# Half a piece of the expert weights per head pair, the rest in and behind the last eight pairs, and row replication moved from the chain into the expert stage: attention followed by soft mixture of experts on one core

## The chip, the core and the metric

The kernel runs on one core of one Trainium2 chip. The metric is device time in microseconds (us). Engines: TensorE (PE; its weight loads are PEld), VectorE (DVE), ScalarE (ACT), GpSimd (POOL), SyncE (SP). Sixteen DMA engines move the data. A profile shows one execution; its span is about 1.8 us shorter than the time of the same run. Runs over 1.5% above the fastest of their kernel count as slow and are left out of ratios.

## The reference

Causal attention over 8 batches x 8 heads of 576 tokens, with 16 beacon keys and values ahead of them; its output, as 4608 rows of 512, goes through a soft mixture of 8 experts with 4 slots each.

```python
scores = scale * np.matmul(q, k_all.transpose(0, 1, 3, 2))     # causal mask, softmax
x = attn_out.transpose(0, 2, 1, 3).reshape(B * S, H * D)       # 4608 x 512
logits = x @ phi                                               # 4608 x 32 slots
d = softmax(logits, axis=0); slot_input = d.T @ x
for e in range(8):                                             # w1: 512 x 1024, w2: 1024 x 512
    slot_out[e] = np.maximum(slot_input[e] @ w1[e], 0) @ w2[e]
out = softmax(logits, axis=1) @ slot_out
```

The slot inputs need all rows of x, so no expert can start before the last head pair is done. The weights are 33.5 MB in 4-byte floats; q, k and v are 9.4 MB each.

## The kernel before

Attention runs over 32 pairs of heads. SyncE issues the loads of q and k, five pairs ahead. GpSimd masks the exponentials, and in the same instruction stream issues the loads of v and of the expert weights, which the transfer casts to 2-byte floats. The weights come in 32 pieces, four per expert (two of w1, then two of w2), each 128 packets of 4096 bytes in SBUF.

```python
def load_w(i):                       # ... source of piece i
    nc.gpsimd.dma_start(out=arena[:, wloc[m]:wloc[m] + WP], in_=src)

for n in range(NP):                  # 32 pairs
    ...                              # scores, exponentials, masks, products, transposes
    want = n if n < 6 else n - (n - 1) // 4 if n < 24 else 18 + 9 * (n - 23) // 5
    while wl < min(want, NPC):
        load_w(wl)
        wl += 1
while wl < NPC:
    load_w(wl)
    wl += 1
```

Each issue on GpSimd waits for the transfer eight places before it, because completions are counted on eight semaphores in turn. Behind the loop stands the tail: the last pair, the logits of the last batch, three memsets on GpSimd that clear padding, the replication of exponentials into all row groups (`spread_rows`, `spread_ends`: products and a copy), the slot inputs (`si_half`), and then the experts, two at a time:

```python
for p in range(EP + 2):              # EP = 4 pairs of experts
    if p < EP:
        first_layer(p)               # 16 products with w1
    ...
    if 0 < p <= EP:
        turn_hidden(p - 1)
    if p > 1:
        second_layer(p - 2)          # 16 products with w2
soh = ...                            # VectorE scales the slot outputs: "the scaling"
```

After the scaling come the output products, two copies out of PSUM and 9.44 MB of stores.

The softmax here doesn't subtract the row's maximum and nothing guards it: scores larger than these inputs give would overflow.

## Time and profile before

| stage (profiled run) | us |
|---|---|
| GpSimd starts its last weight issues (all masking done) | 148.8 |
| last weight packet lands | 162.7 |
| scaling starts | 166.1 |
| span | 194.7 |
| median of the first three runs | 197.3 |

Where a stage is quoted from the trace below, "scaling" is the group `soh<-av,rd` of VectorE, "second-layer products" are `av<-arena,hbuf` of TensorE, and "last weight packet" is the end of the last DMA packet of 4096 bytes in the packet records. Counts of packets, pieces and read rates are sums over the packet records (casts counted double for reads), not lines of a view.

### The profile page before, as it was taken

The page shows a single profiled execution, that of the slowest core. Times are in us where ns is not written, and L with a number is a line of the kernel's source. Part 1 is how long each engine was busy: PE and PEld are TensorE (multiplying, and loading weights), DVE is VectorE, ACT ScalarE, POOL GpSimd, SP SyncE. Part 2 cuts the span into 40 slices and gives each one's busy share as a digit, 9 for nine tenths or more (in the row PEclk, how much of TensorE's full clock was granted, in tenths as well). Part 3 has the DMA queues.
Part 4 walks back from the last instruction along what each step waited for, and adds up shares of the span by engine and source line. Part 5 has one row for each costly group of instructions (what it writes and reads, how often), then busy time and mean ns, then how long its engine had stood idle before and what let it go on. Part 6 is the DMA issues. An engine that isn't in the chain of part 4 may idle for free. (4 is left out here: it accounts for less than half of the span.)

```text
span 194.7 us, 7324 instructions
## 1 busy us (share of the span) xinstructions
PE 156.7 (81%) x3123; PEld 106.8 (55%) x3123; DVE 138.6 (71%) x286; ACT 128.3 (66%) x175; POOL 112.5 (58%) x293
## 2 busy tenths in 40 slices
PE   6778986779999888968999799988878699887400
PEld 2445765646776665646767566656656544454100
DVE  5537697578989888985799699788657342799700
ACT  2697763748997778775889678877795222578500
POOL 8659893945897597778778687666756100000000
PEclk9955899979999999996999999999999889999955
DMA  6999999999999999999999999999999990399994
GB/s 183 264 240 350 271 242 266 280 261 265 311 261 265 260 276 258 278 255 304 272 282 260 255 293 261 256 254 222 211 213 215 213 186 19 105 380 417 416 428 199
DMA packets 20464, 50.84 MB, mean 261 GB/s; under 512 B 5456, under 2 KB 5456, under 8 KB 19408
## 3 DMA queue, kind: packets, MB, share of 16 engines
q0 software_dynamic: 8048, 21.74, 56.3%
q1 hardware_dynamic: 12240, 28.35, 40.6%
q8 instruction: 24, 0.39, 0.8%
q10 hardware_dynamic: 144, 0.29, 0.5%
q14 instruction: 8, 0.07, 0.1%
HBM read 62.65 MB, written 9.44 MB: 370 GB/s over the span
## 5 line engine op out<-in xcount | busy, mean ns | idle before, releaser
L294 ACT ACTIVATE ex<-sc 128x736 f16<-128x736 f32 (+1 forms) x124 | 101.5, 870 | 27.4 <-PE sc L287 25.4
L296 POOL TENSOR_SCALAR_AFFINE_SELECT ex<-ex 128x256 f16<-128x256 f16 (+1 forms) x155 | 57.3, 399 | 31.4 <-ACT ex L294 31.0
L287 PE MATMUL sc<-qT,kT 64*128 64x336 bf16 (+5 forms) x384 | 44.9, 302 | 4.4 <-ACT ex L294 2.1
L309 PEld LDWEIGHTS <-ex 128*128 128x128 f16 (+1 forms) x930 | 37.5, 108 | 16.9 <-issue 14.8
L309 PE MATMUL av<-vh,ex 128*128 128x65 f16 x840 | 39.6, 200 | 6.3 <-issue 3.4
L270 PE MATMUL tr<-idb,arena 64*64 64x64 bf16 x1152 | 32.0, 201 | 6.6 <-DMA arena<-in_k_dram 2.3
L270 PEld LDWEIGHTS <-arena 64*64 64x64 bf16 x1152 | 25.4, 114 | 20.2 <-issue 13.3
L276 DVE COPY kT<-tr 128x576 bf16<-128x576 bf16 x27 | 20.4, 756 | 9.6 <-PE tr L270 9.6
L320 DVE TENSOR_TENSOR xb<-av,r 128x640 f16<-128x640 f32 x31 | 25.6, 825 | 1.1
L276 DVE COPY qT<-tr 128x576 bf16<-128x576 bf16 x32 | 23.2, 725 | 4.0 <-PE tr L270 3.9
L287 PEld LDWEIGHTS <-kT 64*128 64x128 bf16 (+1 forms) x384 | 15.9, 102 | 14.1 <-issue 6.1
L151 DVE STREAM_TRANSPOSE vh<-vbuf 128x256 f32<-128x256 f32 x32 | 20.4, 657 | 3.3 <-DMA vbuf<-in_beacon_v_dram 1.9
L183 POOL DMA_DIRECT2D arena<-in_moe_w_dram x32 | 17.9, 560 | 0.2
L698 ACT ACTIVATE arena<-fp,rc 128x512 f32<-128x512 f32 (+1 forms) x18 | 11.3, 677 | 7.4 <-PE fp L696 5.9
L127 POOL DMA_DIRECT2D vbuf<-in_v_dram x27 | 15.1, 571 | 0.2 <-DVE xb L320 0.2
L340 DVE COPY xT<-tr 128x592 f16<-128x592 f16 x31 | 13.9, 455 | 1.0 <-PE tr L332 1.0
L332 PE MATMUL tr<-idh,xb 128*128 128x128 f16 (+1 forms) x160 | 14.2, 221 | 0.1
L700 DVE TENSOR_SCALAR arena<-fp,rc 128x512 f32<-128x512 f32 (+1 forms) x19 | 13.1, 732 | 1.2 <-PE fp L696 0.4
L696 PE MATMUL fp<-soh,eLh 128*128 128x512 f16 (+1 forms) x37 | 10.6, 373 | 2.5 <-ACT arena L698 1.7
L319 DVE RECIPROCAL r<-av 128x10 f32<-128x10 f32 x31 | 6.8, 218 | 7.9 <-PE av L309 7.5
L332 PEld LDWEIGHTS <-xb 128*128 128x128 f16 (+1 forms) x160 | 10.4, 103 | 1.1 <-issue 0.9
L696 PEld LDWEIGHTS <-eLh 128*128 128x128 f16 x37 | 3.9, 114 | 5.7 <-issue 4.5
(101 smaller groups left out, 135.6 us busy)
## 6 DMA issues: line engine op xcount, KB each, us to landing
arena<-in_moe_w_dram POOLq DMA_DIRECT2D x32, 512.0 KB, 10.0
arena<-in_q_dram SPq DMA_DIRECT2D x32, 288.0 KB, 14.6
arena<-in_k_dram SPq DMA_DIRECT2D x31, 288.0 KB, 14.9
out_dram<-arena SPq DMA_DIRECT2D x8, 1024.0 KB, 7.2
vbuf<-in_v_dram POOLq DMA_DIRECT2D x30, 128.0 KB, 8.4
arena<-in_v_dram POOLq DMA_DIRECT2D x4, 128.0 KB, 8.4
out_dram<-arena SPq DMA_DIRECT2D x2, 256.0 KB, 3.5
out_dram<-arena SPq DMA_DIRECT2D x1, 512.0 KB, 4.0
```

The source lines that it names most:

```text
L127: nc.gpsimd.dma_start(out=vbuf[b % 2][32 * qd:32 * qd + 32, :], in_=bass.AP(tensor=v.tensor, offset=v.offset + lo, ap=[hs_, cs_, [1, TK * ...
L151: nc.vector.transpose(out=dst[:, e], in_=src.bitcast(FP).rearrange("p (j e) -> p e j", j=TK)[:, e])
L183: nc.gpsimd.dma_start(out=arena[:, wloc[m]:wloc[m] + WP], in_=src)
L270: nc.tensor.transpose(tp[po:po + 64, j, :], hi, idb[po:po + 64, po:po + 64])
L276: nc.vector.tensor_copy(out=dst, in_=src)
L287: nc.tensor.matmul(sc[0:kn, a, col:col + un], kT[n % 3][64 * a:64 * a + 64, P * c:P * c + kn], qT[n % 3][64 * a:64 * a + 64, u0:u0 + un], ...
L294: nc.scalar.activation(e, sc[:, :, 0:w], AF.Exp, scale=scale)
L296: nc.gpsimd.affine_select(out=e[0:m, :, o:o + m], in_=e[0:m, :, o:o + m], compare_op=AL.is_ge, fill=0.0, base=0, pattern=[[0, 2], [1, m]], ...
L309: nc.tensor.matmul(dst[0:m, i * DD:(i + 1) * DD], ex[n][0:kn, o + a * w:o + a * w + m], vchunk(b, 2 * g + a, c, kn), start=(c == 0), stop= ...
L320: nc.vector.tensor_tensor(out=xb[b % 2][:, :, 2 * g:2 * g + 2, :].rearrange("p i a d -> p a i d"), in0=avv[:, :, :, 0:D], in1=r5[:, :, :]. ...
L332: nc.tensor.transpose(tp[:, i, 0:m], xb[b % 2][0:m, i, 2 * g:2 * g + 2, :].rearrange("p h d -> p (h d)"), idh[0:m, 0:m])
L696: nc.tensor.matmul(fp_[:, c], etok(cg, j), soh[:, c], start=True, stop=True)
```

## The change

Two parts go together. The weight schedule issues half a piece per pair until pair 23, and the rest in the last eight pairs and behind them; its intent, as I read it, is to leave the transfers to q, k and v while attention runs. The tail moves replication out of the chain ahead of the slot inputs into the first expert pair, adds three idle products, meant to keep TensorE's clock up, and puts half of a small fold ahead of the last transposes.

```diff
-        want = n if n < 6 else n - (n - 1) // 4 if n < 24 else 18 + 9 * (n - 23) // 5
+        want = n // 2 if n < 24 else 12 + 5 * (n - 23) // 4
@@ last pair
-        if rows == (0,):
-            spread_rows(0, nc.vector)
@@ logits of the last batch
     logits(L, lp, [0, 1, 2])
-    fold_si(0)
+    xt_piece(NP - 1)
     fold_si(1)
-    xt_piece(NP - 1)
     logits(L, lp, [3])
     logit_exp(L, lp)
-    spread_rows(1, nc.scalar)
+    spread_rows(0, nc.scalar)
+    warm_tail(3)                     # three 128x512 products, result unused
     ...
-    spread_ends(0, 4, nc.scalar, av[:, 1, 128:128 + 4 * UL])
@@ experts
         if p < EP:
             first_layer(p)
+        if p == 0:
+            spread_ends(0, 4, nc.scalar, av[:, 1, 128:128 + 4 * UL])
+            spread_rows(1, nc.scalar)
```

(`fold_si(0)` now stands right after `xt_piece(NP - 2)`, ahead of the logits.)

More of the change, by code (lines that the diff above doesn't have):

```diff
@@ L602, with warm_tail @@
     lp = scs[1][:, 0, 0:ZW]
+    fold_si(0)
     logits(L, lp, [0, 1, 2])
-    fold_si(0)
+    xt_piece(NP - 1)
     fold_si(1)
-    xt_piece(NP - 1)
     logits(L, lp, [3])
     logit_exp(L, lp)
-    spread_rows(1, nc.scalar)
+    spread_rows(0, nc.scalar)
+    def warm_tail(k):
+        for _ in range(k):
+            nc.tensor.matmul(scs[0][:, 1, :], idh[:, :], xTs[L % 2][:, 0:512],
+                             start=True, stop=True)
+    warm_tail(3)
     dt_piece(L)
```

## The prediction

> **What bounds the kernel now.** I read the page first, then the windows view (busy time of each engine in chosen stretches), the list of DMA issues, the timeline from 149 us on, and last the waits of single instructions. The page gives the engines and three rows over 40 slices of 4.87 us:
>
> ```profile
> PE 156.7 (81%) x3123; PEld 106.8 (55%) x3123; DVE 138.6 (71%) x286; ACT 128.3 (66%) x175; POOL 112.5 (58%) x293
> ...
> DMA  6999999999999999999999999999999990399994
> GB/s 183 264 240 350 271 242 266 280 261 265 311 261 265 260 276 258 278 255 304 272 282 260 255 293 261 256 254 222 211 213 215 213 186 19 105 380 417 416 428 199
> ...
> q0 software_dynamic: 8048, 21.74, 56.3%
> q1 hardware_dynamic: 12240, 28.35, 40.6%
> ```
>
> No engine is full, but the 16 DMA engines are: nine tenths or more in every slice from the second to the 33rd, then a hole of two slices, then the output. q0 (the GpSimd queue) carries v and the expert weights, cast from 4-byte to 2-byte, so the GB/s of the page, which counts bytes written, is half of what is read for them; q1 carries q, k and the output. The windows view gives the stages (the last numbers of a row are the granted clock, the DMA share, and GB/s written):
>
> ```profile
> 60.00:92.00 32.00, 27.06 (x607) 19.52 (x605) 27.06 (x53) 23.48 (x30) 24.73 (x67) 0.95 1.06 272
> 92.00:129.00 37.00, 34.24 (x817) 24.39 (x813) 31.31 (x61) 30.07 (x40) 26.82 (x72) 0.99 1.06 268
> 129.00:149.40 20.40, 17.87 (x392) 12.90 (x385) 14.63 (x30) 16.24 (x21) 14.15 (x38) 1.00 1.06 217
> 149.40:166.10 16.70, 13.98 (x211) 7.60 (x210) 6.62 (x19) 4.37 (x8) 1.42 (x5) 0.90 0.70 142
> 166.10:194.70 28.60, 13.80 (x99) 7.73 (x99) 16.41 (x32) 12.88 (x23) 0.00 (x0) 0.82 0.81 331
> ```
>
> So attention ends near 149 us, the expert stage near 166, and the output is paced by its write (0.92 to 1.02 DMA share from 170 on). Within attention TensorE is busy 85 to 93% and DMA is over 1.0: two limits that nearly coincide. From about 131 us on the queue holds only weights. Counting their 4096-byte packets (128 to a 512 KB piece), ten pieces end between 133.7 and 158.5 us, **2.48 us apiece**. The last of the 32 lands near 160.5 us, 11 us after its issue at 149.4. The timeline shows what then ends the expert stage:
>
> ```profile
> 148.81 1.08 POOL L183 DMA_DIRECT2D arena<-in_moe_w_dram  x2
> ...
> 164.16 1.91 PE L665 MATMUL av<-arena,hbuf 128*32 128x512 f16 x32
> ...
> 166.13 0.88 DVE L684 TENSOR_SCALAR soh<-av,rd 128x256 f16<-128x256 f32 x2 [1.43 <-PE av L665]
> ```
>
> The last second-layer products, which read the last pieces, start at 164.16, 3.7 us after the data is there. The weights are hidden now, with 3 to 4 us to spare; the chain attention, logits, slot inputs, experts sets the end.
>
> **What the Trainium skill says.** Page "DMA: Bandwidth & Descriptors", section "Anatomy of one DMA — SWDGE (gpsimd) path": a GpSimd DMA costs about 2.0 us plus its bytes over 436 GB/s. The trace agrees on the rate, if bytes read are counted: 211 to 213 GB/s written is 422 to 426 read while only weights run. The same section says that any semaphore wait happens on the issuing sequencer before dispatch. That is why the place of an issue in GpSimd's program counts: the trace has each weight issue as 0.55 us of GpSimd's queue, behind the pair's masking. Page "TensorE: Matmul & The Clock Gate", section "Part 1: The HAM clock gate": after an idle window of about 3.4 us the clock falls to half. The trace agrees in kind (0.50 to 0.55 granted between 10 and 20 us), and it will matter if TensorE has to wait for weights.
>
> **The change part by part.**
>
> (a) *Weight schedule.* There are 32 pieces. The code before issues up to n for pairs n below 6, n-(n-1)//4 up to 23, and 18+9(n-23)//5 after: 18 by pair 23, all 32 by pair 31. After: n//2 gives 11 by pair 23, then 12+5(n-23)//4: 13, 14, 15, 17, 18, 19, 20, 22 for pairs 24 to 31, and **10 more behind the last pair**. The instruction order of GpSimd shows it: after the last masking come 12 weight issues in a row (2 of pair 31 and the 10), where before there were 2.
>
> What it removes: 7 pieces of 2.48 us = 17.4 us of DMA work from before pair 24; 3 of them lie before pair 6, where TensorE is busy only 14.9 of 20 us (24 to 44). What it adds: this work comes back at the end, where nothing is left to hide it. Pairs 24 to 30 issue 9 pieces, 22.3 us of DMA in about 28 us, with the last k and q loads as all the rest, so I take it that no backlog is left when the last pair is masked. Then, from the moment T when GpSimd is done masking (148.8 us before):
> - the first of the 12 pieces lands at about T + 0.55 (issue) + 2.0 (the skill's fixed cost, an estimate) + 2.5 = T + 5;
> - the other 11 follow at 2.48 us: 27.3 us. Last landing T + 32.3 us.
>
> With T unmoved that is 181.1. Four products and the start of the scaling by VectorE behind it: 0.5 us, so 181.6 in place of 166.1: **+15.5 us**.
>
> (b) *What attention gains, X.* Less DMA early lets v, k and q land sooner and T come earlier. The waits view has from 24 to 135 us: TensorE and its weight loads behind k and q 5.9 us, VectorE behind v 1.9, GpSimd behind v and phi 2.9; these overlap. Against a large gain: reckoning landings from the packets, q and k of pairs 9 to 30 arrive 5 to 12 us before their transposes, so the steady state is paced by TensorE and ScalarE. I choose **X = 5 us**, 1 to 10 being possible; TensorE's idle time from 24 to 149 us is 16 us in all, which no change of loads can remove whole.
>
> (c) *Rows replicated elsewhere.* Four replication products leave the last attention pair (0.4 us), seven more and two ScalarE copies (0.58 and 0.44 us) leave or move in the chain before the slot inputs, and stand in expert pair 0; three 128x512 warm products come in (about 0.2 us each at full clock), and half of the fold moves ahead of the last transposes. Between 151.5 and 155.4 us the chain could lose some 1 us, above all the 1.11 us that replicated ends wait for GpSimd's memsets. But behind (a) the experts wait for weights 20 us later, so this is worth **0** on the path. One new hazard: those memsets now stand behind the 12 issues. A piece waits for the one eight places before it, so the last issue waits for piece 24, about T + 5 + 3 x 2.48 = T + 12.5, and TensorE, in order, waits in expert pair 0. That is before the last landing at T + 32, and the remaining expert pairs (2.2 us each in the timeline) fit between.
>
> (d) *Output.* Same 9.44 MB at the same rate, 28.6 us from the scaling to the end. TensorE comes out of waits, so its first products may run at half clock: +0.5 us at most, an estimate from 0.37 us mean of an output product times a few.
>
> Sum: 15.5 - 5 + 0 + 0.2 = +10.7 on 197.3, about **208 us**.
>
> **The rivals.**
> 1. *Attention was starved by loads, and the relief pays for it all.* For: DMA share 1.06 through all of attention, TensorE at 75% in 24 to 44 us. Against: k and q land well ahead; X would have to be 14 or more, nearly all TensorE idle time. It would give 193 to 199 us.
> 2. *The weights are hidden anyway.* They have 3.7 us of slack and DMA is work-conserving, so if DMA never idles it still ends near 160.5, the chain gains 1 us of (c) and something of X: 193 to 196 us. Against: q and k have only five buffers, so removed weights can't be replaced by other loads for long; 17.4 us of work removed early leaves holes, and 12 pieces issued at T need 30 us whatever came before.
> 3. *GpSimd's queue is the bound.* The memsets behind 12 issues hold TensorE past the last landing: only if they came after T + 28. Then 210 to 214 us.
>
> **Range and chances.** The 27.3 us of the last 11 pieces are firm to half a microsecond; X is the uncertain term. X from 1 to 10 gives 203 to 212; the runs before spread from 196.0 to 200.3, so I take 202.5 to 212.5. Within 2% would need X of 11 or more: 5%; faster by 2% needs rival 1 or 2 in full: 2%; slower: 93%.
>
> **What would show it.** In the changed profile: (a) GB/s and DMA share under 0.9 in some slices before 140 us, weights alone at about 213 GB/s for some 30 us after attention, last landing near 175; TensorE's expert products waiting for the weight DMA; the hole between loads and output shrinking to some 3 us. (b) The last exponentials of attention near 144 instead of 148. (c) No row copies between the logits' exponential and the slot inputs, memsets some 12 us after the last masking. (d) 28 to 29 us from scaling to end. The prediction is wrong if DMA stays full all through attention, or if attention ends before 138.

## The result

The changed kernel takes 210.74 us (208.0 to 213.5, 4 runs) against 197.15 us: ratio 1.066, interval 1.052 to 1.081, slower. A ratio here is the mean time of one kernel's fast runs over that of the other's fast runs of the same rounds, so it isn't quite the ratio of the medians. The results are correct.

The page of the changed kernel, the same two rows over 40 slices, now of 5.22 us:

```profile
DMA  6999999999999799899999898997999998089994
GB/s 178 263 280 347 289 278 262 286 281 285 204 267 269 176 246 256 227 199 248 275 237 267 236 195 151 187 173 146 185 213 212 213 214 179 25 333 413 414 425 206
```

Before, the DMA row had nothing but nines until the output; now there are sevens and eights from slice 14 on, and slices as low as 146 and 151 GB/s. The stretch of weights alone at 212 to 214 GB/s (211 to 215 before) moved from slices 29 to 32 to slices 30 to 33 here, with longer slices and a later end. The windows view of the same stages (from the last: granted clock, DMA share, GB/s written):

```profile
60.00:92.00 32.00, 28.71 (x675) 20.83 (x673) 27.69 (x53) 25.09 (x33) 24.22 (x68) 0.99 0.94 232
92.00:129.00 37.00, 34.34 (x801) 24.46 (x797) 32.56 (x64) 30.64 (x39) 25.52 (x70) 1.00 1.00 237
149.40:180.00 30.60, 15.02 (x167) 6.29 (x164) 4.56 (x13) 3.40 (x6) 3.59 (x9) 0.67 0.95 191
180.00:208.80 28.80, 15.02 (x99) 8.02 (x98) 16.11 (x32) 13.14 (x23) 0.00 (x0) 0.80 0.80 329
```

In the first two rows the transfers write 232 and 237 GB/s where they wrote 272 and 268, and TensorE is a little busier (28.7 of 32 us against 27.1): attention did gain. In the third row TensorE works 15 of 30.6 us, with the DMA share at 0.95. The last row, the output, is as it was.

Why DMA isn't full any more is told by the waits of SyncE, which issues q and k (us in total, times, longest us). First the kernel before, then the changed one:

```profile
SPq L95 <- DMA arena<-in_q_dram: 25.9, 21, 2.9
SPq L95 <- PE tr L270: 14.3, 12, 2.1
```

```profile
SPq L95 <- PE tr L270: 42.7, 24, 4.1
SPq L95 <- DMA arena<-in_q_dram: 2.3, 4, 1.2
```

The two other large lines, for k and for TensorE's scores (`PE sc L287`), are alike: 24.5 and 14.9 us before, 1.9 and 39.2 us changed. Before, SyncE waited mostly for earlier loads to land (14.6 us from issue to landing for q in the page, 7.0 us changed). With fewer weights in the way it waits for TensorE instead, which has to be done with one of the five buffers. So q and k can't fill the freed time.

The timeline of the changed kernel around the end of the experts:

```profile
145.15 3.73 POOL L183 DMA_DIRECT2D arena<-in_moe_w_dram  x7
...
159.54 0.53 POOL L183 DMA_DIRECT2D arena<-in_moe_w_dram  x1 [1.89 <-DMA arena<-in_moe_w_dram]
160.10 0.20 POOL L616 MEMSET eLh<- 32x128 f16 x1
...
160.70 0.43 PE L367 MATMUL av<-eLh,rept 128*128 128x128 f16 x3 [9.90 <-POOL eLh L617]
...
174.04 0.40 PE L669 MATMUL av<-arena,hbuf 128*32 128x512 f16 x4 [0.59 <-DMA arena<-in_moe_w_dram]
...
176.54 0.40 PE L669 MATMUL av<-arena,hbuf 128*32 128x512 f16 x4 [2.10 <-DMA arena<-in_moe_w_dram]
...
178.95 0.62 PE L669 MATMUL av<-arena,hbuf 128*32 128x512 f16 x4 [2.01 <-DMA arena<-in_moe_w_dram]
...
179.61 0.88 DVE L691 TENSOR_SCALAR soh<-av,rd 128x256 f16<-128x256 f32 x2 [6.89 <-PE av L669]
```

The square bracket tells how long the engine idled before the group, and for whom. Two waits are to be seen. TensorE stood 9.9 us for GpSimd's memsets, which stand behind the twelve weight issues in GpSimd's stream. Later it stood 0.6, 2.1 and 2.0 us for weight pieces, one after the other. The second kind comes last. Which of the two sets the end is a question for an experiment, since the first is the longer.

### The profile page after: what moved, and what is told of

It is laid out like the page before. It is cut to its first block, busy times and chain, and to the rows that moved or that the text cites. A ratio compares the mean times of both kernels' runs of the same rounds, so it can differ in the third digit from the quotient of the medians.

```text
span 208.8 us, 7327 instructions
## 1 busy us (share of the span) xinstructions
PE 160.5 (77%) x3126; PEld 107.4 (51%) x3126; DVE 137.5 (66%) x285; ACT 129.2 (62%) x176; POOL 112.7 (54%) x293
## 5 line engine op out<-in xcount | busy, mean ns | idle before, releaser
L294 ACT ACTIVATE ex<-sc 128x736 f16<-128x736 f32 (+1 forms) x124 | 101.5, 869 | 24.5 <-PE sc L287 23.2
L287 PE MATMUL sc<-qT,kT 64*128 64x336 bf16 (+5 forms) x384 | 44.9, 298 | 4.1 <-ACT ex L294 1.5
L309 PEld LDWEIGHTS <-ex 128*128 128x128 f16 (+1 forms) x930 | 37.0, 107 | 18.2 <-issue 14.4
L309 PE MATMUL av<-vh,ex 128*128 128x65 f16 x840 | 39.0, 199 | 8.0 <-issue 3.1
L270 PE MATMUL tr<-idb,arena 64*64 64x64 bf16 x1152 | 31.3, 200 | 4.0 <-DVE qT L276 1.9
L270 PEld LDWEIGHTS <-arena 64*64 64x64 bf16 x1152 | 25.1, 113 | 16.7 <-issue 10.9
L287 PEld LDWEIGHTS <-kT 64*128 64x128 bf16 (+1 forms) x384 | 16.0, 101 | 13.3 <-issue 4.7
L705 ACT ACTIVATE arena<-fp,rc 128x512 f32<-128x512 f32 (+1 forms) x18 | 11.4, 678 | 13.1 <-PE fp L703 11.3
L707 DVE TENSOR_SCALAR arena<-fp,rc 128x512 f32<-128x512 f32 (+1 forms) x19 | 13.2, 733 | 2.1 <-PE fp L703 1.3
L703 PE MATMUL fp<-soh,eLh 128*128 128x512 f16 (+1 forms) x37 | 11.6, 415 | 2.3 <-ACT arena L705 1.7
L367 PEld LDWEIGHTS <-rept 128*128 128x128 f16 x41 | 3.2, 108 | 12.1 <-issue 11.0
```

The costliest lines, as they stand in the source:

```text
L270: nc.tensor.transpose(tp[po:po + 64, j, :], hi, idb[po:po + 64, po:po + 64])
L287: nc.tensor.matmul(sc[0:kn, a, col:col + un], kT[n % 3][64 * a:64 * a + 64, P * c:P * c + kn], qT[n % 3][64 * a:64 * a + 64, u0:u0 + un], ...
L294: nc.scalar.activation(e, sc[:, :, 0:w], AF.Exp, scale=scale)
L309: nc.tensor.matmul(dst[0:m, i * DD:(i + 1) * DD], ex[n][0:kn, o + a * w:o + a * w + m], vchunk(b, 2 * g + a, c, kn), start=(c == 0), stop= ...
```

## The experiments

My theory: the schedule takes transfer work away from a time when the DMA engines have no other work to fill in, and the same work then stands behind the last pair, where nothing hides it. The scaling comes a fixed short time behind the last weight packet. Rivals: the tail costs the time; GpSimd's stream holds TensorE (the 9.9 us); the position of the ten issues behind the last pair counts, not the work put off; attention was starved by loads and should have won far more.

### Schedule alone, tail alone

e1 is the kernel before with the one line of the schedule changed:

```diff
-        want = n if n < 6 else n - (n - 1) // 4 if n < 24 else 18 + 9 * (n - 23) // 5
+        want = n // 2 if n < 24 else 12 + 5 * (n - 23) // 4
```

> The weight schedule alone, with the tail of the kernel before. My theory (the ten pieces behind the last pair set the end): as slow as the whole change, 208 to 213 us, last weight packet about 33 us after GpSimd starts its closing issues, and first scaling by VectorE 1 us behind it. In the old tail the replicated ends stand ahead of the slot inputs, so TensorE will wait there for the memsets until about 160 us and do all experts after that, but should still be done before the last piece. Rival (the rearranged tail costs the time): near 197 us.

Measured: 210.16 us, ratio 1.072 (1.062 to 1.082). The schedule alone costs all of it. In the old tail the slot inputs also wait for the memsets, as the waits and the timeline of e1 show:

```profile
PE av L367 <- POOL eLh L612: 10.9, 1, 10.9
...
178.30 0.62 PE L665 MATMUL av<-arena,hbuf 128*32 128x512 f16 x4 [1.83 <-DMA arena<-in_moe_w_dram]
178.96 0.88 DVE L684 TENSOR_SCALAR soh<-av,rd 128x256 f16<-128x256 f32 x2 [8.07 <-PE av L665]
```

TensorE lost 10.9 us ahead of all experts and still stood waiting for the last pieces at the end.

e2 is the changed kernel with the old line of the schedule (the same edit the other way round).

> The rearranged tail alone, with the old weight schedule. My theory: it shortens the chain from the last logits to the first expert pair by about 1 us and the weights do not bind, so 195.5 to 197 us, ratio to before 0.99 to 1.00; the scaling starts at about 165 us instead of 166.1. Rival (moved copies cost as much in the expert pairs): same as before or up to 1 us slower. If the tail were the cause of the loss: over 205 us.

Measured: 195.03 us, ratio 0.987 (0.976 to 0.999); its profile fell in a slow run (mean clock 0.74, with 0.75 granted where the others have 1.0). The tail is a small gain, not the loss.

### Memsets off GpSimd

e3 takes the 9.9 us wait away and leaves all else of the changed kernel:

```diff
-    nc.gpsimd.memset(eLz[64:96, :, 4, UL - 64:32], 0.0)      # and two more
+    nc.vector.memset(eLz[64:96, :, 4, UL - 64:32], 0.0)
```

> The changed kernel with its three closing memsets on VectorE instead of behind twelve weight issues on GpSimd. Theory: TensorE's wait of 9.9 us for these memsets disappears from the trace, the experts run earlier and wait for the weights instead, and the time stays within 1% of the changed kernel, 208 to 213 us. Rival (GpSimd's queue holds the end): 5 to 10 us faster than the changed kernel, 200 to 205 us.

Measured: 210.4 us, ratio 1.068 (1.057 to 1.079), against 1.066 of the changed kernel. In its profile, which is of a slow run, the memsets run at 149.3 us and TensorE no longer waits for them; a product for the column sums waits for GpSimd's copy of the fold instead (9.2 us), which the move left behind the issues. The last packet still lands 34.8 us after the closing issues begin, and the scaling follows 0.97 us behind it. So e3 swapped one wait for GpSimd against another and doesn't rule its stream out by itself; nor does e4 below, where GpSimd is free early too. The timelines do: in the changed kernel TensorE, released by GpSimd at 160.7 us, still stood 4.7 us in all for weight pieces, the last until 178.95 us; and in e5 GpSimd had done its last work at 153.2 us, 18 us before the scaling.

### The suspected cause taken away

e4 gives a wrong result: the last ten pieces aren't loaded, and the experts that would read them read pieces loaded ten places earlier.

```diff
-    while wl < NPC:
-        load_w(wl)
-        wl += 1
+    for i in range(wl, NPC):
+        wloc[worder[i]] = wloc[worder[i - 10]]
```

> Wrong result on purpose: the changed kernel without its last ten weight loads; the experts that would read them read pieces loaded ten places earlier. It takes the suspected cause away and keeps all the arithmetic. Theory: the scaling starts about 16 us after the last masking, near 161 us, and the time is 191 to 194 us, 3 to 6 us under the kernel before, which is what attention gained plus 1 us of the tail. Rival (something else in the change lengthens the chain): 200 us or more.

Measured: 192.14 us, ratio 0.976 (0.967 to 0.986), relative error 0.82. Its timeline:

```profile
146.28 1.08 POOL L183 DMA_DIRECT2D arena<-in_moe_w_dram  x2
...
161.76 0.88 DVE L690 TENSOR_SCALAR soh<-av,rd 128x256 f16<-128x256 f32 x2 [1.43 <-PE av L668]
```

Without those ten loads the scaling comes 15.5 us after the closing issues begin instead of 34.5. All the arithmetic and all the other issues are still there. The ten pieces cost 18.6 us in the medians (210.74 less 192.14), on other chips, so take it as about 18.

### Work put off, or place behind the last pair

e5 keeps the lean schedule until pair 23 but issues all other 21 pieces within the last eight pairs.

```diff
-        want = n // 2 if n < 24 else 12 + 5 * (n - 23) // 4
+        want = n // 2 if n < 24 else 11 + 21 * (n - 23) // 8
```

> The changed kernel with its half-a-piece-per-pair schedule up to pair 23 (11 pieces), but all other 21 pieces issued in the last eight pairs, none behind. It tells whether the ten issues behind the last pair cost the time, or the transfer work that was put off. Theory (work put off, transfers then at one piece in 2.47 us): 21 pieces from about 116 us last till about 170, scaling near 171, time 201 to 205 us, ratio 1.02 to 1.04, so about half of the loss stays though nothing is issued behind the last pair. Rival (the position behind the last pair is what costs): 194 to 197 us.

Measured: 203.67 us, ratio 1.037 (1.018 to 1.057); last packet at 170.7, scaling at 171.7 us. Nothing stands behind the last pair in program order, and half of the loss is still there, so the position isn't the whole cost. GpSimd's issues now wait for their eighth predecessor, from 141.9 us on (the last starts at 151.6 us), so the transfers decide when they can be made. The other half went, and the packet records show how: all of q and k has landed by 119.3 us in the changed kernel and by 117.7 us in e5, and from 119.3 us to the closing issues the weights were then read at 337 GB/s in the changed kernel, which asks for too few, and at 423 GB/s in e5. So 9.4 pieces instead of 12.6 were left at the end. In both kernels it is the work still left after attention that costs.

### How much attention can gain

e7 loads no weight at all until the last pair is done (`want = 0`).

> The changed kernel with no weight loaded before the last pair is done: all 32 behind it. It measures how early attention can end with no weights beside it, the most that relief can give. Theory: attention is then paced by TensorE and ScalarE, and GpSimd is done masking at 141 to 145 us against 148.8 before; the 32 pieces last 79 us more, time 252 to 260 us. Rival (attention is starved by loads): masking done before 135 us.

Measured: 250.97 us in one run; all masking is done at 137.2 us, better than I expected but short of the rival's 135. The windows of e7:

```profile
60.00:92.00 32.00, 29.74 (x710) 21.66 (x706) 29.74 (x59) 26.75 (x34) 24.15 (x68) 1.00 0.75 186
92.00:129.00 37.00, 35.94 (x864) 26.48 (x863) 33.77 (x64) 32.73 (x42) 21.97 (x63) 1.00 0.40 102
```

TensorE is busy 97% of 92 to 129 us (93% before), with DMA at 0.40. So the weights slow attention by 11.6 us in all (148.8 to 137.2, one profile each); the changed schedule won back 3.7 of these, and to win all 11.6 costs 82 us of weights at the end. Which of attention's waits the weights lengthen I didn't pin down: the profile before shows only a few microseconds of waits for q, k and v.

### The clock of TensorE

In five profiles (changed kernel, e1, e5, e7, e8) TensorE waits for the last weight pieces, and its granted clock is at half when the scaling starts; there the span ends 29.2 to 29.3 us after the scaling (28.9 in the slow run of e3). In those with the full clock at the scaling (before, e4, e6, e10, e11) it is 28.2 to 28.7. e8 adds four idle products ahead of each of the last three groups of second-layer products, e9 eight:

```diff
         for z in range(4):
+            if p == EP - 1 and z > 0:
+                warm_tail(8)                     # e8: 4
```

> The changed kernel with four idle products of 128x512 ahead of each of the last three groups of second-layer products, which wait for weights about 2 us each. It tests whether TensorE's lowered clock after these waits costs the output anything. Theory: scaling starts at the same distance from the last packet (1 us or less), the clock of the first output products is back at full, and the distance from the scaling to the end falls from 29.2 to about 28.6 us. Rival (clock has no part in it): 29.2 stays.

> As the run with four idle products ahead of each wait, but eight: there the granted clock still fell to 0.50 ahead of the output and the distance from scaling to end stayed 29.3 us, so that run could not tell. Eight products at full clock fill about 1.7 us of each 2.47 us. If the clock stays at 1.0 into the output and the distance falls to about 28.6 us, the lowered clock is what costs the 0.6 us; if the clock stays at 1.0 and the distance is still 29.2 us or more, it is not; if the clock falls again, it stays open.

e8 (one look, 207.96 us) told nothing, because the clock still fell. e9 (one look, 211.62 us) did tell. The windows of e8, then of e9, around the scaling, at 176.9 and 181.7 us (first number after the stretch: TensorE busy; third from the end: granted clock):

```profile
174.00:176.00 2.00, 1.14 (x8) 0.40 (x5) 0.00 (x0) 0.00 (x0) 0.00 (x0) 0.97 0.45 90
176.00:178.00 2.00, 1.20 (x7) 0.49 (x7) 0.88 (x2) 0.14 (x1) 0.00 (x0) 0.50 0.00 0
```

```profile
178.00:180.00 2.00, 2.00 (x12) 0.83 (x12) 0.00 (x0) 0.00 (x0) 0.00 (x0) 1.00 0.55 111
182.00:184.00 2.00, 1.67 (x14) 1.08 (x14) 1.57 (x4) 1.14 (x3) 0.00 (x0) 1.00 0.00 0
```

In e9 the clock stays at 1.0 and the end comes 28.2 us after the scaling, 1.0 us less than in the changed kernel. So the lowered clock accounts for the extra half microsecond or more; but the idle products delay the scaling to 1.39 us behind the last packet (0.98 in the changed kernel), so 0.6 us is left. Against a loss of 13.6 us this is small. e9 as a whole wasn't faster than the changed kernel.

### A version that is faster than both

e6 uses the new tail and is lean at the start only, with the old totals at pairs 23 and 31. Its first comparison fell on a chip where even the kernel before spread from 194.6 to 207.2 us, so I ran it again as e11, beside the tail alone as e10.

```diff
-        want = n // 2 if n < 24 else 12 + 5 * (n - 23) // 4
+        want = n // 2 if n < 8 else 3 + 15 * (n - 7) // 16 if n < 24 else 18 + 9 * (n - 23) // 5
```

> The rearranged tail with a schedule that is lean only at the start: half a piece per pair up to pair 7 (3 pieces instead of 6), then 15 pieces in 16 pairs, so 18 by pair 23 and 32 by pair 31 as in the kernel before. Theory: transfers stay full, the last packet stays near 162.7 us, attention ends 1 to 3 us earlier, scaling near 164 us, time 193 to 195.5 us, ratio to before 0.97 to 0.99. Rival (even three pieces put off leave a hole): last packet after 165 us and no gain on the 195.0 us of the tail alone.

> The rearranged tail with the old weight schedule once more, on one chip with the lean start, because the first comparison of the lean start fell on a chip with a wide spread. Expected as before: ratio 0.98 to 0.995 to the kernel before.

> The lean start once more. In its first profile attention lost near pair 31, waiting for q and k, what it had gained in the first eight pairs, and the scaling came at 165.4 us against 165.6 of the tail alone. Theory now: with transfers full throughout, fewer weights at the start and more in the middle give nothing, so the same as the tail alone within 1%. Rival (lean start helps, the first comparison was noise): 1% or more under the tail alone.

Measured: e6 199.41 us, ratio 1.008 (0.970 to 1.047), inconclusive. e10 194.53 us, ratio 0.985 (0.979 to 0.992). e11 195.82 us, ratio 0.989 (0.983 to 0.996). The tail with the old schedule has the lowest time of all that are correct, 1.5% under the kernel before; the lean start adds nothing that can be seen, as the two intervals overlap. The timeline of e10 shows what comes next:

```profile
147.40 1.08 POOL L183 DMA_DIRECT2D arena<-in_moe_w_dram  x2
...
150.21 0.30 ACT L353 ACTIVATE eLh<-sc 128x160 f16<-128x160 f32 x1 [1.59 <-PE sc L346]
...
162.93 0.40 PE L669 MATMUL av<-arena,hbuf 128*32 128x512 f16 x4 [0.91 <-DMA arena<-in_moe_w_dram]
...
163.38 0.88 DVE L691 TENSOR_SCALAR soh<-av,rd 128x256 f16<-128x256 f32 x2 [2.52 <-PE av L669]
```

With a chain 1.3 us shorter than before from the last issues to the scaling (16.0 against 17.3 us), TensorE now stands 0.9 us for the very last piece, whose last packet lands at 162.55 us. The windows of e10 show that the DMA engines as a whole aren't full until then (last two numbers: DMA share, GB/s):

```profile
156.00:158.00 2.00, 2.00 (x40) 0.93 (x36) 0.50 (x2) 0.60 (x1) 0.00 (x0) 1.00 1.07 217
158.00:160.00 2.00, 2.00 (x37) 0.72 (x29) 0.42 (x1) 0.60 (x1) 0.00 (x0) 1.00 0.62 125
160.00:162.50 2.50, 2.02 (x36) 0.97 (x33) 0.42 (x1) 0.00 (x0) 0.00 (x0) 1.00 0.16 31
```

The packet records have only two packets under way in the last 1.5 us, where some 16 are usual: most of the engines have nothing left to do. No order of the loads gains much on the full stretch up to 158 us, but these last microseconds might be won by other means; that wasn't tried. In e11 the last products stand 0.5 us for the last piece as well. There the transposes of pair 31 had waited 1.9 us for k (0.7 us in e10), which landed at 137.1 us (136.9 in e10), so what the lean start had gained was lost again:

```profile
137.75 0.69 PE L270 MATMUL tr<-idb,arena 64*64 64x64 bf16 x18 [1.91 <-DMA arena<-in_k_dram]
```

### All runs in one table

The rows are profiled runs, one each; "issues" is when GpSimd starts the closing weight issues, "left" the pieces still to land then, counted in packets.

| kernel | issues | left | last packet | scaling | scaling less last packet | scaling to end |
|---|---|---|---|---|---|---|
| before | 148.8 | 4.8 | 162.7 | 166.1 | 3.4 | 28.6 |
| changed | 145.2 | 12.6 | 178.6 | 179.6 | 0.98 | 29.2 |
| e1 schedule alone | 144.0 | 12.7 | 178.0 | 179.0 | 0.99 | 29.3 |
| e2 tail alone (slow run) | 148.1 | 4.8 | 162.7 | 165.6 | 2.9 | 28.6 |
| e3 memsets moved (slow run) | 145.4 | 12.8 | 180.2 | 181.2 | 0.97 | 28.9 |
| e4 ten pieces lent | 146.3 | 2.6 | 155.1 | 161.8 | 6.6 | 28.2 |
| e5 all by last pair | 146.7 | 9.4 | 170.7 | 171.7 | 1.01 | 29.3 |
| e6 lean start | 149.5 | 4.9 | 164.6 | 165.4 | 0.77 | 28.6 |
| e7 weights last | 137.2 | 32.0 | 219.1 | 220.1 | 0.98 | 29.2 |
| e8 four idle products | 143.1 | 12.6 | 175.9 | 176.9 | 0.99 | 29.3 |
| e9 eight idle products | 147.4 | 12.5 | 180.3 | 181.7 | 1.39 | 28.2 |
| e10 tail alone again | 147.4 | 5.0 | 162.6 | 163.4 | 0.83 | 28.4 |
| e11 lean start again | 148.4 | 5.2 | 163.1 | 163.9 | 0.82 | 28.7 |

In every kernel that put work off, the scaling follows the last packet by 1.0 us, wherever that packet falls between 170.7 and 219.1 us; only the eight idle products of e9 make it 1.4. In e6, e10 and e11, with the full clock at the end, it is 0.8. In e4, before and e2, the chain is the later one.

## Why the prediction was right, by its own steps

The prediction, 208 us in 202.5 to 212.5, holds the measured 210.7. Its mechanism is shown by e1 (the schedule alone costs all), e4 (without the ten loads the loss is gone) and e5 (with 9.4 pieces left in place of 12.6, half of the loss).

- **What bounds the kernel.** Two readings were off. The last q and k packets land at 135.2 us, not 131. And I took the last landing before as near 160.5 us, at the pace of the pieces ahead of it; the packet records have it at 162.7, so the slack was 2.4 us against a chain that follows at 1.0, not 3.7. The last piece is complete 4.6 us after the one ahead of it, counted in packets, because only one or two packets are under way at the end. This showed only in e10, where the shorter chain at once ran into the weights.
- **(a) The schedule.** Predicted: last landing 32.3 us after the closing issues begin. Measured: 33.5. Counted in packets, the first of the twelve is complete 4.7 us after the issues begin (predicted 5), though 12.57 pieces were left and not 12; the next ten follow 2.47 us apart, as predicted; the last comes 4.0 us behind its forerunner. That slow end makes up the miss of 1.2 us. From the last packet to the scaling it was 0.98 us, not 0.5.
- **(b) What attention gains.** Predicted 5 us, measured 3.7 (148.8 to 145.2). Each of these is one profile. Six profiles of this schedule have the closing issues begin between 143.1 and 147.4 us, three of the old one between 147.4 and 148.8, so 5 isn't excluded and a miss of 1.3 us can be chance. Rival 1 was half right about the possible size, since e7 gives 11.6 us; why half a piece per pair collects so little of it isn't shown.
- **(c) The tail.** On the path of the changed kernel it is worth nothing, as predicted, and the hazard I named was there: the last issue comes 14.4 us after the first (estimated 12.5), and TensorE waits for the memsets behind it until 160.7 us. By itself the tail is worth 1.3 to 1.5% (e2, e10), 2.5 to 3 us where I said 1. In the profile of e10 1.3 us of these are the shorter chain; 1.4 us are closing issues that begin earlier, which can be chance. Part of its gain lies ahead of the logits' exponential (2.8 us from the last issues in e10 against 4.1 before), part behind it, where I had named the 1.11 us wait: the first expert products start 1.65 us after that exponential against 2.44 before. In e10 the wait of 0.9 us for the last piece takes this second part back, so from exponential to scaling it is 13.2 us in both; e4, which doesn't wait, has 12.5.
- **(d) The output.** 29.2 us after the scaling against 28.6; I allowed 0.5 for the clock but put 0.2 in the sum.

The misses add up: 1.3 in (b), 1.2 and 0.5 in (a), 0.4 in (d) make 3.4 us, and the spans differ by 14.1 us where the sum said 10.7. All four went the same way; the range was drawn for X alone, so that the other misses fitted into it is partly luck.

Rival 2 (weights are hidden anyway) failed where the prediction said it would: the read rate of all loads between 60 and 92 us, from the packet records with cast packets counted double, fell from 395 to 316 GB/s. That freed time was not refilled is what the waits of SyncE show. Rival 3 fell with the timelines (changed kernel and e5): GpSimd's memsets were late, but never last.

## What to carry to other kernels

When the transfers are full from beginning to end, a load that is put off is not saved: look at what the queue would do in the freed time, and if q and k can't run further ahead because their buffers are full, the freed time is a hole that comes back at the end. Weigh it as pieces left at the end of the stage that hides them, times the time of one piece alone in the queue; here 7.8 more pieces of 2.46 us against 3.7 us won and 2.4 us of slack, 13.1 us, where the scaling came 13.5 us later. And before judging a long wait by its length, see whether another wait ends after it: TensorE's 9.9 us for GpSimd's memsets set nothing, and the 2.0 us for the last piece set the end.

## What the Trainium skill lacked or had wrong

- "DMA: Bandwidth & Descriptors", section "Anatomy of one DMA — SWDGE (gpsimd) path", puts most of the 2 us of fixed cost into the write receipt behind the last byte. For loads into SBUF the runs show 0.30 to 0.38 us from the end of the last packet to the start of the products that waited for it (178.62 to 178.95 us in the changed kernel, 170.66 to 171.01 in e5), unless the packet's own time already holds the receipt.
- The same page, section "Where 436 GB/s comes from", says that about 358 GB/s binds between HBM and SBUF. With one core at work the weights alone were read at 422 to 430 GB/s (211 to 215 written, cast from 4 to 2 bytes), which agrees with the page's own 425 for large transfers of a single core. So the page has the right number elsewhere, and only this sentence, read alone, misleads.
- "Perfetto Trace Analysis", section "DMA Engine Tracks", says that a DMA engine's slices show actual busy time. In 60 to 92 us of the changed kernel the mean GpSimd packet of 4096 bytes took 363 ns against 325 before, with the same median (324 and 322), so the DMA share fell only from 1.06 to 0.94 while the read rate fell by 20%. Bytes per second show such holes better than the busy share; what lengthens these packets isn't shown.
- "TensorE: Matmul & The Clock Gate", section "HAM oscillation — how this bites in real kernels", gives as the abstract rule no idle gaps over some 3.4 us. Here the clock fell without such gaps. In e8 it fell to 0.50 at 175.9 us; since its return to full at 165.6 us the longest gap of TensorE had been 1.1 us, but in the last 3.41 us it had been busy only 46% of the time. In e9, busy without a gap until the last piece, it stayed at 1.0. In the kernel before it fell at 10.5 us with no gap over 0.54 us in the 3.41 us ahead of that, so the half clock there (until 20.7 us) is no case of an idle window. In the changed kernel's wait of 9.9 us it fell after 2.3 us. In twelve profiles (all but that of e2) the granted clock changed only at steps of 3.41 us. The 55 such stretches at full clock that were followed by a fall had TensorE busy 72% at most; the 501 others had it busy 61% at least, but for three in e3's slow run (50 to 57%). That points to the busy share of the stretch rather than to the length of a gap.
